# Reordering the opening of a fused transformer kernel: one transposing transfer ahead of two loads, one tile centred by halves

## The chip, the cores and the metric

The kernel runs on one core of one Trainium2 chip. The metric is the device time of one execution in microseconds (us). The granted TensorE clock was 1.0 in every run but one, a run at 0.998. A profiled execution gives a span about 2 us shorter than its time (1290.4 against 1292.35 for the profiled run of the kernel before).

Engines: PE is TensorE, DVE is VectorE, ACT is ScalarE, SP is the engine that issues all transfers here. "SPq" in a timeline is SP issuing a transfer; the transfer itself lands later.

## The reference, cut to what matters

Four layers over one activation of 2048 rows by 1024: attention, token-mixing MLP, attention, MLP.

```
x = x + A(layernorm(x), wqkv, wo)     # layer 1: V = layernorm(x) @ wqkv[:, 2048:3072], then Q, K, ...
x = x + B(layernorm(x), w1, b1, w2, b2)
x = x + A(layernorm(x), wqkv, wo)
x = x + B(layernorm(x), w1, b1, w2, b2)
```

The change touches only the first 35 us: load x in 16 tiles of 128 rows (256 KB each), normalise each, transpose each, and multiply by the V weights.

## The kernel before: the parts that matter

Each engine gets a list of work in a fixed order. `x_load k` loads tile k, `w_load kt` loads weight row kt of the V weights (256 KB), `S_`/`A_`/`R_`/`N_` take the statistics of a tile, its reciprocal root and normalise it, `M_`/`Ma` only centre it (tiles 0 and 1, whose scale is applied later), `tr` transposes on TensorE, `C_` copies the result from PSUM to `hT`, `T_ k` is a transposing transfer from the normalised tile into `hT`, `V_` is the projection, `E_` evicts it. `VV(k, kt, ...)` is the projection of tile k with the named weight rows alone, and `W_` is a matmul on dummy data.

```python
def T_(k):
    return nc.sync.dma_start_transpose(out=hT[:, :, cols(*order[k])], in_=xs[k])
...
pe = [(tr, 0, 0), (tr, 0, 1), (W_, 1), *VV(0, 0), (tr, 1, 0), (tr, 1, 1), *VV(0, 1, 2), *VV(1, 0, 1, 2)]
for kt in range(3, 6):
    pe += [*VV(0, kt), *VV(1, kt)]
pe += [(tr, 2, 0), (tr, 2, 1), *VV(0, 6, 7), *VV(1, 6, 7)]
pe += [(V_, k, n, a8) for k in range(2, NT) for n in range(NDC)]
act = [(Ma, 0, halves[1]), (C_, 0, 0), (C_, 0, 1), (C_, 1, 0), (C_, 1, 1), (R_, 0), (R_, 1), (R_, 2), (R_, 3), (C_, 2, 0),
       (C_, 2, 1), (R_, 4), (E_, 0), (R_, 5), (E_, 1), (R_, 6), (E_, 2), (E_, 3)]
rs = [(R_, k) for k in range(7, NT)]
for k in range(4, NT):          # E_4, R_7, R_8, E_5, R_9, R_10, E_6, ...
    act.append((E_, k))
    act += rs[:2]
    del rs[:2]
dve = [..., (S_, 1, 0), (S_, 1, 1), (A_, 1), (M_, 1, whole[0]), (S_, 2, 0), (S_, 2, 1), (A_, 2)]
...                             # then per tile k: S_ k+1 (first half), N_ k, S_ k+1 (second half), A_ k+1
sp = [(x_load, 0, halves), (x_load, 1), *((w_load, kt) for kt in range(4)), (x_load, 2), (w_load, 4), (w_load, 5),
      (x_load, 3), (w_load, 6), (w_load, 7), (x_load, 4), (x_load, 5), (x_load, 6), (T_, 3), (x_load, 7), (x_load, 8),
      (T_, 4), (x_load, 9), (x_load, 10), (x_load, 11), (T_, 5), (x_load, 12), (x_load, 13), (T_, 6), (x_load, 14),
      (x_load, 15), (T_, 7), (T_, 8), (T_, 9), (T_, 0), (T_, 1), *((T_, k) for k in range(10, NT)), (load_biases,)]
```

The softmax here doesn't subtract the row's maximum and nothing guards it: scores larger than these inputs give would overflow.

Of the kernel before, what the change touches and what calls it, by code (L numbers as in the profile page):

```python
# [25 lines left out]
def kernel(  # L26
# [177 lines left out]
    def chain_(eng, f, *args):  # L204
        with tc.issue_after(last[eng].ins) if eng in last else nullcontext():
            last[eng] = f(*args)

    def start_up(v, wv):
        xc = [x2(f"xc{k}") for k in range(2)]
        xs, tps, pss_, mvs, sts, rss = {}, {}, {}, {}, {}, {}  # L210
# [22 lines left out]
        def B_(k):  # L233
            return nc.vector.tensor_scalar(out=nm0[:], in0=mvs[k][:, 0:1], scalar1=-1.0, scalar2=None, op0=ALU.mult)

        def M_(k, h):
            return nc.vector.tensor_scalar(out=xc[k][:, h], in0=xs[k][:, h], scalar1=mvs[k][:, 0:1], scalar2=None,
                                           op0=ALU.subtract)

        def Ma(k, h):  # L240
            return nc.scalar.activation(out=xc[k][:, h], in_=xs[k][:, h], func=ACT.Identity, bias=nm0[:])

        def R_(k):
# [48 lines left out]
        halves = (slice(0, D // 2), slice(D // 2, D))  # L292
        whole = (slice(0, D),)
        chain_("ACT", ln_exp_table)
        def VV(k, *kts):
            return [(V_, k, n, [kt]) for kt in kts for n in range(NDC)]

        a8 = range(KD)
        pe = [(tr, 0, 0), (tr, 0, 1), (W_, 1), *VV(0, 0), (tr, 1, 0), (tr, 1, 1), *VV(0, 1, 2), *VV(1, 0, 1, 2)]
        for kt in range(3, 6):  # L300
            pe += [*VV(0, kt), *VV(1, kt)]
        pe += [(tr, 2, 0), (tr, 2, 1), *VV(0, 6, 7), *VV(1, 6, 7)]
        pe += [(V_, k, n, a8) for k in range(2, NT) for n in range(NDC)]
        act = [(Ma, 0, halves[1]), (C_, 0, 0), (C_, 0, 1), (C_, 1, 0), (C_, 1, 1), (R_, 0), (R_, 1), (R_, 2), (R_, 3), (C_, 2, 0),
               (C_, 2, 1), (R_, 4), (E_, 0), (R_, 5), (E_, 1), (R_, 6), (E_, 2), (E_, 3)]
        rs = [(R_, k) for k in range(7, NT)]
        for k in range(4, NT):
            act.append((E_, k))
            act += rs[:2]
            del rs[:2]  # L310
        dve = [(S_, 0, 0), (S_, 0, 1), (A_, 0), (B_, 0), (M_, 0, halves[0]), (S_, 1, 0), (S_, 1, 1), (A_, 1), (M_, 1, whole[0]),
               (S_, 2, 0), (S_, 2, 1), (A_, 2)]
        for k in range(2, NT):
            nx = k + 1 < NT
# [8 lines left out]
            if k in (8, 9):  # L323
# [1 line left out]
        dve.append((zero_fill,))  # L325
        dve.append((cast_biases,))
        sp = [(x_load, 0, halves), (x_load, 1), *((w_load, kt) for kt in range(4)), (x_load, 2), (w_load, 4), (w_load, 5),
              (x_load, 3), (w_load, 6), (w_load, 7), (x_load, 4), (x_load, 5), (x_load, 6), (T_, 3), (x_load, 7), (x_load, 8),
              (T_, 4), (x_load, 9), (x_load, 10), (x_load, 11), (T_, 5), (x_load, 12), (x_load, 13), (T_, 6), (x_load, 14),
              (x_load, 15), (T_, 7), (T_, 8), (T_, 9), (T_, 0), (T_, 1), *((T_, k) for k in range(10, NT)), (load_biases,)]  # L330
        qs = {"PE": pe, "ACT": act, "DVE": dve, "SP": sp}
        need = {cast_biases: lambda: (load_biases,) in done, R_: lambda k: k in mvs, N_: lambda k, h: k in rss, tr: lambda k, hf: (N_, k) in done if k > 1 else (M_ if k or not hf else Ma, k) in done,
                S_: lambda k, cc: (x_load, k) in done,
                B_: lambda k: k in mvs, M_: lambda k, h: k in mvs, Ma: lambda k, h: (B_, k) in done, C_: lambda k, hf: (k, hf) in tps,
                V_: lambda k, n, kts: ((C_, k, kts[-1] * 2 // KD) in done or (T_, k) in done), E_: lambda k: (V_, k, 1) in done and (k > 1 or k in rss),
                T_: lambda k: (N_, k) in done and (k > 1 or (E_, k) in done)}
        done = set()
        while any(qs.values()):
            for eng, q in qs.items():
                while q and (q[0][0] not in need or need[q[0][0]](*q[0][1:])):  # L340
                    f, *args = q.pop(0)
                    chain_(eng, f, *args)
                    if f is V_:
                        if args[2][-1] == KD - 1:
                            done.add((f, args[0], args[1]))
                    else:
                        done.add((f, *(args if f is C_ else args[:1])))

    def load_wv():
        return [wt_("wv", [P, 2, D]) for _ in range(KD // 2)]  # L350
# [280 lines left out]
    for li in range(2):  # L631
# [5 lines left out]
        if first:  # L637
            start_up(v, wv)
            wts = [None, None]
            chain_("SP", load_qk, 0, wts)  # L640
            res = lambda c, i: xin_v[c, i]
        else:
            fill_wv(wv)
            wts = [None, None]
            chain_("SP", load_qk, 0, wts)
            for i in range(NI):
                for c in range(DIL):
                    v_proj(v, c, i, wv, (0, 1))
            res = lambda c, i: rows(xb, c, i)
# [104 lines left out]
```

## Time and profile before

| | kernel before |
|---|---|
| median time before the prediction, 3 runs | 1292.2 us (1292.11 to 1293.29) |
| profiled span | 1290.4 us |
| TensorE busy | 1285.0 us |
| TensorE idle before tile 1's transposes | 0.75 us |
| TensorE idle before tile 4's projection | 0.64 us shown; 0.80 us counted from 22.05, where 32 matmuls of 0.216 us after 15.14 end |

The page of the profile says what limits the kernel. These are the first lines of its first part (busy time, share, number of instructions) and of the chain of waits that ended last:

```profile
span 1290.4 us, 19531 instructions
PE 1285.0 (100%) x8422; PEld 591.8 (46%) x8422; DVE 417.4 (32%) x854; ACT 368.7 (29%) x609; POOL 2.4 (0%) x15
...
PE 98%; DMA 1%; DVE 0%; SPq 0%; ACT 0%; issue 0%
```

TensorE is busy all the time, so a reordering can win only its idle time, 5.4 us, of which most is at the very start and the very end. The Trainium skill ("Perfetto Trace Analysis", section "Identifying the Most-Contended Engine") warns that matmul busy time does not say how near a kernel is to its roofline; it is enough here, since the change removes no matmul and only gaps can move.

The timeline of TensorE before. Columns: start, duration, engine, line, operation, output <- inputs, shape, count, and in brackets the idle time before it and what ended it:

```profile
7.76 0.62 PE L256 MATMUL m<-ident,xc 128*128 128x128 bf16 x8 [0.75 <-DVE xc L237]
...
15.14 7.07 PE L267 MATMUL s<-wv,hT 128*128 128x512 bf16 x32
22.85 3.63 PE L267 MATMUL acc<-wv,hT 128*128 128x512 bf16 x16 [0.64 <-DMA hT<-x]
26.31 7.07 PE L267 MATMUL s<-wv,hT 128*128 128x512 bf16 x32
33.22 3.62 PE L267 MATMUL acc<-wv,hT 128*128 128x512 bf16 x16
...
64.30 7.07 PE L375 MATMUL m<-hT,wqk 128*128 128x512 bf16 x32
```

The line at 7.76 is tile 1's transposes, 15.14 is tiles 2 and 3, 22.85 is tile 4, 26.31 tiles 5 and 6, 33.22 tile 7, and 64.30 the first matmul of the Q/K projection. The two gaps are in brackets.

The same stretch of SP, as it issues loads (DMA_DIRECT2D, L218) and transposing transfers (L279):

```profile
14.86 1.36 SPq L279 DMA_TRANSPOSE hT<-x  x1
16.28 1.05 SPq L218 DMA_DIRECT2D x<-in_A_x_dram  x2
17.43 1.24 SPq L279 DMA_TRANSPOSE hT<-x  x1
...
23.93 1.24 SPq L279 DMA_TRANSPOSE hT<-x  x1
25.21 1.08 SPq L218 DMA_DIRECT2D x<-in_A_x_dram  x2
28.56 18.66 SPq L279 DMA_TRANSPOSE hT<-x  x11
```

A duration here is the time SP spends issuing. The Trainium skill says so ("Perfetto Trace Analysis", section "DMA Instruction — HWDGE (DVE, Sync)"): the profiled window ends when the issuer is free, and the data's movement is not in it. This trace agrees: tile 4's transfer shows 1.24 us from 17.43, and its data landed 5.4 us after that start. The view of one tile (here the transfers into `hT` that were issued in a short window around 17.43) gives the landing:

```profile
L279 SPq DMA_TRANSPOSE hT<-x x1: 1237/1237/1237, 17.4 to 17.4; - x1
...
DMA to landing us min/median/max: 5.4/5.4/5.4
```

17.43 and 5.4 make 22.8, which is where TensorE resumes. The same view around 28.56 gives tile 7's transfer in the kernel before; it matters later:

```profile
L279 SPq DMA_TRANSPOSE hT<-x x1: 1238/1238/1238, 28.6 to 28.6; - x1
...
DMA to landing us min/median/max: 3.1/3.1/3.1
```

It landed at 31.7, and TensorE reached tile 7 at 33.22: 1.5 us to spare.

### The profile page before, as it was taken

How to read it: one execution, taken by the hardware profiler on the slowest of the kernel's cores; microseconds unless marked ns; L12 is line 12 of the kernel's file. 1: busy time of each engine (PE TensorE's matmuls, PEld its weight loads, DVE VectorE, ACT ScalarE, POOL GpSimd, SP SyncE). 2: the span in 40 equal slices, each digit the busy share in tenths (PEclk: the TensorE clock that was granted, in tenths of full speed). 3: DMA queues.
4: the chain of work that ended last, by engine and by line, in shares of the span. 5: the costliest groups of instructions: out<-in, count | busy, mean ns of one | idle time of the engine just before them, and what ended most of it. 6: DMA issues, size and time to landing. Idle time of an engine off the chain costs nothing.

```text
span 1290.4 us, 19531 instructions
## 1 busy us (share of the span) xinstructions
PE 1285.0 (100%) x8422; PEld 591.8 (46%) x8422; DVE 417.4 (32%) x854; ACT 368.7 (29%) x609; POOL 2.4 (0%) x15
## 2 busy tenths in 40 slices
PE   9999999999999999999999999999999999999999
PEld 4444444444444444444444444444444444444444
DVE  6566777820000022322300677678000000111111
ACT  4366664541111110000023666645311111000000
POOL 0000000000000000000000000000000000000000
PEclk9999999999999999999999999999999999999999
DMA  8611124642222244465410111247323222334330
GB/s 240 112 46 48 50 83 124 208 139 82 66 82 75 57 117 132 131 164 132 131 32 1 48 49 51 80 151 218 116 67 91 72 62 81 102 106 136 118 92 33
DMA packets 204102, 126.59 MB, mean 98 GB/s; under 512 B 44272, under 2 KB 183792, under 8 KB 204016
## 3 DMA queue, kind: packets, MB, share of 16 engines
q1 hardware_dynamic: 204016, 125.35, 34.3%
q8 instruction: 66, 1.08, 0.4%
q14 instruction: 20, 0.16, 0.0%
HBM read 96.48 MB, written 16.78 MB: 88 GB/s over the span
## 4 chain that ended last, share of the span: by engine, by line
PE 98%; DMA 1%; DVE 0%; SPq 0%; ACT 0%; issue 0%
PE m L375 18%; PE s L617 15%; PE s L570 15%; PE m L490 9%; PE acc L570 7%; PE acc L617 7%; PE m L570 7%; PE m L617 7%; PE m L360 4%; PE s L267 2%; PE s L406 2%; PE acc L441 1%; PE acc L267 1%; PE acc L445 1%; DMA x<-in_A_x_dram 0%; DMA hT<-x 0%
## 5 line engine op out<-in xcount | busy, mean ns | idle before, releaser
L617 PEld LDWEIGHTS <-w 128*128 128x128 bf16 x1820 | 177.0, 98 | 210.2
L570 PEld LDWEIGHTS <-w 128*128 128x128 bf16 x1792 | 175.4, 98 | 211.4
L375 PE MATMUL m<-hT,wqk 128*128 128x512 bf16 x1024 | 231.8, 380 | 0.0
L570 PE MATMUL s<-h,w 128*128 128x512 bf16 x896 | 202.9, 379 | 0.0
L617 PE MATMUL s<-g,w 128*128 128x512 bf16 (+1 forms) x924 | 201.6, 374 | 0.0
L619 DVE SCALAR_TENSOR_TENSOR xo<-s,b_sb,xs 128x512 bf16<-128x512 f32 (+1 forms) x33 | 24.4, 739 | 532.9 <-PE s L617 528.7
L375 PEld LDWEIGHTS <-wqk 128*128 128x128 bf16 x1024 | 95.2, 98 | 118.0 <-issue 10.7
L421 DVE TENSOR_TENSOR Pm<-pc,band 32x640 bf16<-32x640 bf16 x256 | 123.6, 483 | 56.2 <-ACT pc L409 49.3
L490 PE MATMUL m<-wo,oT 128*128 128x512 bf16 x512 | 111.5, 379 | 0.0
L570 PE MATMUL acc<-h,w 128*128 128x512 bf16 x448 | 103.9, 379 | 0.0
L617 PE MATMUL acc<-g,w 128*128 128x512 bf16 x448 | 100.6, 379 | 0.0
L570 PE MATMUL m<-h,w 128*128 128x512 bf16 x448 | 99.0, 379 | 0.0
L617 PE MATMUL m<-g,w 128*128 128x512 bf16 (+1 forms) x448 | 97.8, 376 | 0.0
L178 ACT ACTIVATE ln<-mv,eps 128x1 f32<-128x1 f32 x64 | 18.8, 294 | 228.7 <-DVE mv L186 184.9
L490 PEld LDWEIGHTS <-oT 128*128 128x128 bf16 x512 | 49.6, 98 | 60.4 <-issue 1.3
L577 ACT ACTIVATE g<-s,b_sb 128x1024 bf16<-128x1024 f32 x28 | 31.2, 1113 | 158.2 <-PE s L570 158.2
L386 DVE COPY qB<-qs 32x512 bf16<-32x512 bf16 x136 | 38.2, 281 | 95.3 <-ACT qs L382 94.0
L360 PE MATMUL m<-wv,hT 128*128 128x512 bf16 x256 | 55.4, 379 | 0.0
L409 ACT ACTIVATE pc<-s,shift 128x640 bf16<-128x640 f32 x64 | 51.1, 799 | 11.7 <-PE s L406 11.7
L382 ACT CAST qs<-m 128x512 bf16<-128x512 f32 x64 | 37.4, 585 | 48.4 <-PE m L375 48.4
L379 ACT CAST kT<-m 128x512 bf16<-128x512 f32 x64 | 37.5, 586 | 46.5 <-PE m L375 46.5
L497 DVE TENSOR_TENSOR xn<-m,xr 128x512 bf16<-128x512 f32 x64 | 44.2, 690 | 16.9 <-PE m L490 16.8
(67 smaller groups left out, 678.9 us busy)
## 6 DMA issues: line engine op xcount, KB each, us to landing
w<-in_B_w_dram SPq DMA_DIRECT2D x56, 512.0 KB, 3.8
w<-in_B_w_dram SPq DMA_DIRECT2D x64, 448.0 KB, 4.4
wqk<-in_A_wqkv_dram SPq DMA_DIRECT2D x16, 512.0 KB, 4.8
xa<-xn SPq DMA_DIRECT2D x32, 256.0 KB, 2.2
xs<-xa SPq DMA_DIRECT2D x32, 256.0 KB, 3.1
wo<-in_A_wo_dram SPq DMA_DIRECT2D x8, 512.0 KB, 5.4
xr<-in_A_x_dram SPq DMA_DIRECT2D x16, 256.0 KB, 3.3
xb<-xo SPq DMA_DIRECT2D x16, 256.0 KB, 2.7
```

The costliest lines, as they stand in the source:

```text
L267: r = nc.tensor.matmul(pss_[k][:, n, :], lhsT=hT[:, kt, cols(*order[k])], rhs=wv[kt // 2][:, kt % 2, n * 512:(n + 1) * 512], start=(kt == ...
L360: nc.tensor.matmul(ps[:], lhsT=hT[:, kt, cols(c, i)], rhs=wv[kt // 2][:, kt % 2, n * 512:(n + 1) * 512], start=(kt == 0), stop=(kt == KD - 1))
L375: mm = nc.tensor.matmul(ps[:], lhsT=wts[part][:, kt, (g % 2) * P:(g % 2 + 1) * P], rhs=hT[:, kt, lo:lo + 512], start=(kt == 0), stop=(kt = ...
L379: nc.scalar.copy(out=kT[u % 2][:, ls], in_=ps[:])
L382: nc.scalar.copy(out=qs[:], in_=ps[:])
L386: nc.vector.tensor_copy(out=qB[u % 2][hp, h, ls], in_=qs[hp, :])
L409: nc.scalar.activation(out=pc[:].rearrange("p (n t) h k -> p n (t h k)", n=2), in_=ss[:, :, 0:2 * HG * GW], func=ACT.Exp, scale=scale, bia ...
L421: mm = nc.vector.tensor_tensor(out=Pm[rp, :, s0:s0 + HB, r * KG:r * KG + GW].rearrange("p h t k -> p t h k"), in0=pc[rp], in1=mk, op=ALU.mult)
L490: mm = nc.tensor.matmul(ps[:], lhsT=oT[g][:, cols(c, i)], rhs=wo[n][g // 4][:, g % 4, :], start=(g == 0), stop=(g == NG - 1))
L497: return nc.vector.tensor_tensor(out=xn[:, xs_], in0=pss_["o", n][:], in1=xr[:, xs_], op=ALU.add)
L570: nc.tensor.matmul(pairs[fl][0][dc], lhsT=wt[c][:, i, fl * P:(fl + 1) * P], rhs=h2[c][i][:, dc * 512:(dc + 1) * 512], start=(k == 0), stop ...
L617: nc.tensor.matmul(ap, lhsT=w2t[ft // HF][:, ft % HF, c::DIL], rhs=g[ft // GF][:, ft % GF, lo:lo + w], start=(ft == 0), stop=(ft == FT - 1))
```

## The change

The intent: close both gaps. Tile 4's transposing transfer goes right behind tile 3's, ahead of two loads, and the later loads are regrouped. Tile 1 is centred in two halves, so that its transposes can start after the first, and two matmuls of tile 0 are put ahead of the transposes to fill the gap.

```diff
-        pe = [(tr, 0, 0), (tr, 0, 1), (W_, 1), *VV(0, 0), (tr, 1, 0), (tr, 1, 1), *VV(0, 1, 2), *VV(1, 0, 1, 2)]
+        pe = [(tr, 0, 0), (tr, 0, 1), (W_, 1), *VV(0, 0, 1), (tr, 1, 0), (tr, 1, 1), *VV(0, 2), *VV(1, 0, 1, 2)]
-        dve = [..., (A_, 1), (M_, 1, whole[0]), ...
+        dve = [..., (A_, 1), (M_, 1, 0), (M_, 1, 1), ...
-              ... (x_load, 6), (T_, 3), (x_load, 7), (x_load, 8),
-              (T_, 4), (x_load, 9), (x_load, 10), (x_load, 11), (T_, 5), (x_load, 12), (x_load, 13), (T_, 6), (x_load, 14),
-              (x_load, 15), (T_, 7), (T_, 8), ...
+              ... (x_load, 6), (T_, 3), (T_, 4), (x_load, 7),
+              (x_load, 8), (x_load, 9), (T_, 5), (x_load, 10), (x_load, 11), (T_, 6), (x_load, 12), (x_load, 13), (x_load, 14),
+              (x_load, 15), (T_, 7), (T_, 8), ...
 # cut: M_ and Ma take the number of a half, and the bookkeeping of what is done knows halves
```

More of the change, by code (lines that the diff above doesn't have):

```diff
@@ L234, in B_, with M_, Ma @@
             return nc.vector.tensor_scalar(out=nm0[:], in0=mvs[k][:, 0:1], scalar1=-1.0, scalar2=None, op0=ALU.mult)
-        def M_(k, h):
+        def M_(k, hf):
+            h = halves[hf]
             return nc.vector.tensor_scalar(out=xc[k][:, h], in0=xs[k][:, h], scalar1=mvs[k][:, 0:1], scalar2=None,
                                            op0=ALU.subtract)
-        def Ma(k, h):
+        def Ma(k, hf):
+            h = halves[hf]
             return nc.scalar.activation(out=xc[k][:, h], in_=xs[k][:, h], func=ACT.Identity, bias=nm0[:])
@@ L303, in start_up @@
         pe += [(V_, k, n, a8) for k in range(2, NT) for n in range(NDC)]
-        act = [(Ma, 0, halves[1]), (C_, 0, 0), (C_, 0, 1), (C_, 1, 0), (C_, 1, 1), (R_, 0), (R_, 1), (R_, 2), (R_, 3), (C_, 2, 0),
+        act = [(Ma, 0, 1), (C_, 0, 0), (C_, 0, 1), (C_, 1, 0), (C_, 1, 1), (R_, 0), (R_, 1), (R_, 2), (R_, 3), (C_, 2, 0),
                (C_, 2, 1), (R_, 4), (E_, 0), (R_, 5), (E_, 1), (R_, 6), (E_, 2), (E_, 3)]
@@ L310, in start_up @@
             del rs[:2]
-        dve = [(S_, 0, 0), (S_, 0, 1), (A_, 0), (B_, 0), (M_, 0, halves[0]), (S_, 1, 0), (S_, 1, 1), (A_, 1), (M_, 1, whole[0]),
+        dve = [(S_, 0, 0), (S_, 0, 1), (A_, 0), (B_, 0), (M_, 0, 0), (S_, 1, 0), (S_, 1, 1), (A_, 1), (M_, 1, 0), (M_, 1, 1),
                (S_, 2, 0), (S_, 2, 1), (A_, 2)]
@@ L327, in start_up @@
         sp = [(x_load, 0, halves), (x_load, 1), *((w_load, kt) for kt in range(4)), (x_load, 2), (w_load, 4), (w_load, 5),
-              (x_load, 3), (w_load, 6), (w_load, 7), (x_load, 4), (x_load, 5), (x_load, 6), (T_, 3), (x_load, 7), (x_load, 8),
-              (T_, 4), (x_load, 9), (x_load, 10), (x_load, 11), (T_, 5), (x_load, 12), (x_load, 13), (T_, 6), (x_load, 14),
+              (x_load, 3), (w_load, 6), (w_load, 7), (x_load, 4), (x_load, 5), (x_load, 6), (T_, 3), (T_, 4), (x_load, 7),
+              (x_load, 8), (x_load, 9), (T_, 5), (x_load, 10), (x_load, 11), (T_, 6), (x_load, 12), (x_load, 13), (x_load, 14),
               (x_load, 15), (T_, 7), (T_, 8), (T_, 9), (T_, 0), (T_, 1), *((T_, k) for k in range(10, NT)), (load_biases,)]
         qs = {"PE": pe, "ACT": act, "DVE": dve, "SP": sp}
-        need = {cast_biases: lambda: (load_biases,) in done, R_: lambda k: k in mvs, N_: lambda k, h: k in rss, tr: lambda k, hf: (N_, k) in done if k > 1 else (M_ if k or not hf else Ma, k) in done,
+        need = {cast_biases: lambda: (load_biases,) in done, R_: lambda k: k in mvs, N_: lambda k, h: k in rss, tr: lambda k, hf: (N_, k) in done if k > 1 else (M_, k, hf) in done,
                 S_: lambda k, cc: (x_load, k) in done,
-                B_: lambda k: k in mvs, M_: lambda k, h: k in mvs, Ma: lambda k, h: (B_, k) in done, C_: lambda k, hf: (k, hf) in tps,
+                B_: lambda k: k in mvs, M_: lambda k, hf: k in mvs, Ma: lambda k, hf: (B_, k) in done, C_: lambda k, hf: (k, hf) in tps,
                 V_: lambda k, n, kts: ((C_, k, kts[-1] * 2 // KD) in done or (T_, k) in done), E_: lambda k: (V_, k, 1) in done and (k > 1 or k in rss),
@@ L346, in start_up @@
                     else:
-                        done.add((f, *(args if f is C_ else args[:1])))
+                        done.add((M_ if f is Ma else f, *(args if f in (C_, M_, Ma) else args[:1])))
     def load_wv():
```

## The prediction

> **What bounds the kernel.** The page's first part has TensorE busy 1285.0 of 1290.4 us, clock 1.0; the chain of waits is 98% TensorE. Only its idle time can be removed by a reordering. The timeline shows all of it: 1.05 us at the start, 0.15 and 0.08 us around the first transposes, 0.75 us before tile 1's transposes (7.01 to 7.76, released by VectorE's centring), 0.64 us before tile 4's first projection matmul (22.85, released by the transposing DMA), and 2.65 us after the last matmul. The change aims at the last two of the opening: at most 1.4 us, 0.1% of the run.
>
> **Part 1, tile 4's transfer.** Tile 4 is normalised at 16.27+0.55 = 16.82, but its transfer is issued at 17.43, behind two loads that start issuing at 16.28, and takes 5.4 us to land (22.80). Tile 3's, on an idle queue, took 3.2 us (14.86 to 18.06). The Trainium skill, "DMA: Bandwidth & Descriptors", section "Queues, rings and completion order", says each DMA engine consumes its descriptors in ring order; the 5.4 against 3.2 us agrees: tile 4 queued behind 512 KB of loads. Changed: issue near 16.87, landing at 20.1 to 20.6. TensorE needs it at about 21.7 (below), so the wait goes entirely. TensorE really stood from 22.05 (32 matmuls of 0.216 us from 15.14) to 22.85: 0.80 us.
>
> **Part 2, tile 1.** The two moved matmuls need weight row 1: issued 2.67, landed 4.2 later, 6.87; they run 6.9 to 7.35 inside the gap. The first half of the centring (0.34 us, as tile 0's half took) ends at 7.56 rather than 7.71, so the transposes start near 7.60; the second half ends near 7.85. Two halves cost VectorE about 0.15 us more, harmless: it then waits until 9.57 for tile 2. ScalarE's copy of the first half ends near 8.6, so tile 1's matmuls start near 8.67, not 9.08: 0.4 us gained, with a new stop of about 0.15 us. Weights 3 to 7 (landing 8.4 to 12.8) and tile 2's normalisation (12.25) still come in time. Tile 2's copy follows tile 3's reciprocal root on ScalarE (13.72 to 14.25) and cannot start before 14.16; tile 2's matmuls therefore start near 14.78 instead of 15.14: 0.36 us survives.
>
> **Sum.** Alone, part 2 would be worth nothing, since tile 4's landing absorbs it. With part 1, tile 4's matmuls start near 14.78+6.91 = 21.7, not 22.85: 1.15 us gained.
>
> **Given back?** Tile 5's transfer issues near 19.7 (before 21.48), lands near 24.2; needed at 25.1. Tile 7's load now lands near 22.4, not 19.6, and VectorE's statistics for it stand before tile 6's normalisation: tile 6's transfer slips to near 23.4, lands near 27.5; needed at 28.6. Tile 7 follows ScalarE's eviction of tile 4, which itself is earlier. So no new wait, with about 1 us to spare. After that TensorE has no gap until the end, and the gain is carried to it.
>
> **Predicted:** 1291.1 us, range 1290.5 to 1292.0. Faster by over 2%: 0.005; within 2%: 0.99; slower by over 2%: 0.005.
>
> **Signs.** Timeline: no idle before tile 4's matmuls, which start near 21.7; tile 4's transfer issued near 16.9, landing 3.2 to 3.8 us later; the 0.75 us gap split into about 0.3 us and a small stop before tile 1's matmuls; the V projection ends near 63.1 instead of 64.3; the groups' means unchanged.
>
> **What would make it wrong.** Tile 4's transfer landing after 21.7; tile 3's (18.06) coming after TensorE's earlier need at 18.24; weight row 1 landing later than 7.0, so that the moved matmuls delay tile 1's transposes; tile 5 or 6 landing late because the loads were pushed behind; or run-to-run spread (1292.11 to 1293.29 before) as large as the gain.

## The result

| | before | changed |
|---|---|---|
| median of 6 runs | 1292.35 us (1292.11 to 1293.29) | 1292.49 us (1291.95 to 1293.31) |
| profiled span | 1290.4 us | 1289.9 us |

The ratio is 1.0001, with a 95% interval of 0.9988 to 1.0014: the same. Ratios in this document are the mean time of one kernel's fast runs over that of the other's of the same rounds, so not quite the ratio of the medians quoted. The prediction was 1291.1, and the median lies outside its range of 1290.5 to 1292.0.

The first part of the profile's page after:

```profile
span 1289.9 us, 19532 instructions
PE 1285.3 (100%) x8422; PEld 592.0 (46%) x8422; DVE 417.6 (32%) x855; ACT 369.2 (29%) x609; POOL 2.4 (0%) x15
```

The timeline of TensorE after, for the same pieces of work as above:

```profile
7.41 0.61 PE L258 MATMUL m<-ident,xc 128*128 128x128 bf16 x8
...
14.65 7.08 PE L269 MATMUL s<-wv,hT 128*128 128x512 bf16 x32
21.57 3.62 PE L269 MATMUL acc<-wv,hT 128*128 128x512 bf16 x16
25.02 7.07 PE L269 MATMUL s<-wv,hT 128*128 128x512 bf16 x32
32.64 3.63 PE L269 MATMUL acc<-wv,hT 128*128 128x512 bf16 x16 [0.55 <-DMA hT<-x]
...
63.73 7.07 PE L377 MATMUL m<-hT,wqk 128*128 128x512 bf16 x32
```

Both gaps are gone, and tile 4 starts at 21.57 instead of 22.85, 1.28 us sooner: a little better than predicted. But a new line is in brackets. Tile 7 (32.64) waits for its transposing transfer, which it did not do before. It could have started 32 matmuls of 0.216 us after 25.02, at 31.93. So 0.71 us of the 1.28 is given back there, and 0.57 us (64.30 to 63.73) is left in this trace.

SP and the landing of tile 7's transfer after:

```profile
14.73 3.22 SPq L281 DMA_TRANSPOSE hT<-x  x2
18.00 2.60 SPq L218 DMA_DIRECT2D x<-in_A_x_dram  x3
...
23.16 1.24 SPq L281 DMA_TRANSPOSE hT<-x  x1
24.45 2.08 SPq L218 DMA_DIRECT2D x<-in_A_x_dram  x4
27.27 17.78 SPq L281 DMA_TRANSPOSE hT<-x  x11
```

```profile
L281 SPq DMA_TRANSPOSE hT<-x x1: 1244/1244/1244, 27.3 to 27.3; - x1
...
DMA to landing us min/median/max: 5.3/5.3/5.3
```

Tile 7's transfer is issued 1.29 us sooner than before (27.27 against 28.56), as foreseen, but it lands 5.3 us after that instead of 3.1, at 32.6 instead of 31.7. The four loads just ahead of it (24.45 to 26.53) are the suspect. Note that the same nine loads, of tiles 7 to 15, stand ahead of tile 7's transfer in both lists. What differs is when they land: the last at 30.1 before, 1.5 us ahead of the transfer's own landing, and at 31.7 after. One reason can be read off the times of SP: it issues in order, tile 4's transfer had to wait for its tile until 16.71, and so the load of tile 7 behind it was issued at 18.00 instead of 16.28.

### The profile page after: what moved, and what is told of

It reads as the page before. It is cut to its first block, busy times and chain, and to the rows that moved or that the text cites. A ratio compares the mean times of both kernels' runs of the same rounds, so it can differ in the third digit from the quotient of the medians.

```text
span 1289.9 us, 19532 instructions
## 1 busy us (share of the span) xinstructions
PE 1285.3 (100%) x8422; PEld 592.0 (46%) x8422; DVE 417.6 (32%) x855; ACT 369.2 (29%) x609; POOL 2.4 (0%) x15
## 4 chain that ended last, share of the span: by engine, by line
PE 99%; DMA 1%; DVE 0%; ACT 0%; issue 0%
PE m L377 18%; PE s L619 15%; PE s L572 15%; PE m L492 9%; PE acc L619 7%; PE acc L572 7%; PE m L572 7%; PE m L619 7%; PE m L362 4%; PE s L269 2%; PE s L408 2%; PE acc L269 1%; PE acc L443 1%; PE acc L447 1%; DMA hT<-x 0%; DMA x<-in_A_x_dram 0%
## 5 line engine op out<-in xcount | busy, mean ns | idle before, releaser
L499 DVE TENSOR_TENSOR xn<-m,xr 128x512 bf16<-128x512 f32 x64 | 44.2, 690 | 16.9 <-PE m L492 16.8
```

Source lines behind the costliest of these rows:

```text
L499: return nc.vector.tensor_tensor(out=xn[:, xs_], in0=pss_["o", n][:], in1=xr[:, xs_], op=ALU.add)
```

## The experiments

Theory: in the changed order tile 7's transfer stands behind four loads that were issued just before it, and it lands when they have. Rivals: the transfer is late because what it waits for on ScalarE is late; the total traffic of the opening is the limit, whatever the order; or the first trace was a lucky or unlucky one.

Twelve experiments ran in three batches, each batch beside the kernel before on a chip of its own (nine runs of before in each batch: medians 1292.56, 1292.39 and 1292.25). All twelve were correct.

### 1. The transfers alone

```diff
 # pe, dve as in the kernel before; sp as in the change
```

> Only the order of the transfers is the change's; tile 1 as before. My theory (tile 7's transfer now queues behind four loads and lands near 32.6 us whatever TensorE does): tile 4's matmuls start near 22.1 with no wait for its transfer, tile 7's matmuls still start near 32.6 to 33.0 with 0.2 to 0.6 us of wait for the transfer; the Q/K projection starts 63.7 to 64.1 (before 64.30, the change 63.73); time 0.2 to 0.6 us under before. Rival (tile 7's transfer is late only because tile 4's eviction and the root behind it are late, with a fixed 5.3 us of landing): its landing moves with tile 4's matmuls, to 33.1 or later.

Measured: median 1292.03 (1291.42 to 1293.03), ratio 0.9997 [0.9984, 1.0009]. The profiled run was its slowest, span 1291.0:

```profile
21.47 3.62 PE L267 MATMUL acc<-wv,hT 128*128 128x512 bf16 x16
...
33.80 3.63 PE L267 MATMUL acc<-wv,hT 128*128 128x512 bf16 x16 [1.61 <-ACT v L276]
```

The wait at tile 7 is there without the tile 1 part. The bracket names ScalarE, but the eviction that tile 7 needs (of tile 4, which used the same buffer) was over at 26.13; a wait for several semaphores is put down to whatever the profile saw last. The landing says what it was:

```profile
L279 SPq DMA_TRANSPOSE hT<-x x1: 1247/1247/1247, 27.2 to 27.2; - x1
...
DMA to landing us min/median/max: 6.6/6.6/6.6
```

27.2 and 6.6 make 33.8. The transfer was issued 0.1 us sooner than in the change and landed 1.2 us later, so a fixed landing time behind a late issue is excluded. My numbers missed on both sides: tile 4 started at 21.47 rather than 22.1, and tile 7 later than 33.0.

### 2. Tile 1 alone

```diff
 # pe, act, dve as in the change; sp as in the kernel before
```

> Only tile 1's part of the change (halves, two matmuls ahead); transfers in the order of before. My theory: tile 2's matmuls start near 14.65 instead of 15.14, but tile 4's wait for its transfer grows from 0.64 to about 1.1 us and its matmuls start at 22.7 to 22.9 as before; Q/K projection from 64.2 to 64.3; time equal to before within 0.2 us. Rival (the tile 1 part is worth 0.5 us by itself): Q/K projection from 63.8, time 0.5 us less.

Measured: median 1292.81 (1292.49 to 1293.18), ratio 1.0003 [0.999, 1.0015]. TensorE:

```profile
14.91 7.08 PE L269 MATMUL s<-wv,hT 128*128 128x512 bf16 x32
23.17 3.63 PE L269 MATMUL acc<-wv,hT 128*128 128x512 bf16 x16 [1.18 <-DMA hT<-x]
```

As the theory had it, what is gained before tile 2 is lost again at tile 4, whose transfer landed at 23.1 and whose wait grew from 0.64 to 1.18 us. Alone, this part is worth nothing. The numbers missed here too: tile 2 started at 14.91 and not near 14.65, and tile 4 at 23.17, later than expected and later than before.

### 3 and 9. The change again, twice

> The changed kernel once more, five rounds beside before on one chip, to see whether the 0.5 us of the trace shows in the times and whether tile 7's wait returns. Theory: wait of 0.4 to 1.0 us before tile 7's matmuls at 32.4 to 32.9, Q/K projection from 63.6 to 64.0, time 0.5 us under before, interval about 0.1% wide, so not told from equal. Rival (the trace was a lucky one): no gain in a second trace, Q/K projection at 64.2 or later.

> The changed kernel a third time. Theory (all that differs between runs lies ahead of tile 7's matmuls; span minus the start of those was 1257.2 to 1257.3 us in all ten traces so far): span = that start + 1257.2; wait at tile 7 of 0.5 to 1.7 us; times spread over 1 us or more; mean 0 to 0.7 us under before. Rival (noise sits elsewhere, in the long part after): the difference leaves 1257.1 to 1257.4.

Measured: third run of the list, median 1291.64 (1291.19 to 1292.65), ratio 0.9994 [0.9981, 1.0008]; ninth, median 1292.21 (1291.10 to 1293.43), ratio 1.0002 [0.9988, 1.0016]. In both traces tile 7 waits, and starts at 33.06 and 32.89. The brackets name other releasers again, so the landing was looked up: 33.0 and 32.8. The second trace is less good than I expected: tile 7 at 33.06 rather than up to 32.9, Q/K projection at 64.16 rather than up to 64.0, just short of the rival's 64.2. The five times beside it are 0.6 us under before in the mean, those of the ninth 0.2 us over, where I had expected 0 to 0.7 under.

Span minus the start of tile 7's matmuls is 1257.24 and 1257.21 here, and lies between 1257.18 and 1257.26 in all fourteen traces. So nothing that differs between these kernels, or between profiled runs of one kernel, happens after the start of tile 7. With that, the span of each unprofiled run gives an estimate of when tile 7 started: from 31.8 to 34.0 us over 15 of the change's 16 runs. (The run at clock 0.998 is left out: its later part need not have taken 1257.2 us.) The times spread by 2.3 us (1291.10 to 1293.43), and their mean (the first six, and five each here) is 1292.32, or 1292.24 without that run; the mean of the 24 runs of before beside them is 1292.40. Nothing was won that stands clear of this spread.

### 4. Two of the four loads behind tile 7's and 8's transfers

```diff
-(T_, 6), (x_load, 12), (x_load, 13), (x_load, 14), (x_load, 15), (T_, 7), (T_, 8), (T_, 9),
+(T_, 6), (x_load, 12), (x_load, 13), (T_, 7), (T_, 8), (x_load, 14), (x_load, 15), (T_, 9),
```

> The changed kernel with the loads of tiles 14 and 15 issued behind the transfers of tiles 7 and 8, so two loads stand between tile 6's and tile 7's transfers and not four. My theory (loads ahead in the queue): tile 7's transfer lands 3.2 to 4.0 us after issue at 27.3, by 31.3; TensorE goes from tile 6 to tile 7 at 31.9 with no wait; Q/K projection from 63.0; profiled span 1289.2, time 1.1 to 1.3 us under before. Rival (bytes only moved about: the chain of transfers is bound by throughput to 32.5): tile 7 still waits 0.5 us, Q/K projection from 63.7.

Measured: median 1291.38 (1291.14 to 1291.75), ratio 0.9992 [0.9979, 1.0005]. Tile 7's transfer landed 4.7 us after 27.29 (expected 3.2 to 4.0), at 32.0, and tile 7 started at 32.45 without a wait:

```profile
21.59 3.62 PE L269 MATMUL acc<-wv,hT 128*128 128x512 bf16 x16
25.24 7.37 PE L269 MATMUL s<-wv,hT 128*128 128x512 bf16 x32
32.45 3.62 PE L269 MATMUL acc<-wv,hT 128*128 128x512 bf16 x16
```

The gain is 1.04 us in the means of this batch. But it is smaller than it could be in this trace. Tile 5 starts 0.2 us late (16 matmuls after 21.59 end at 25.04), and the 32 matmuls of tiles 5 and 6 take 7.37 us, not 7.07: tile 6's transfer, behind two loads issued just before, landed 5.2 us after 23.74, when TensorE was already there. So those transfers have next to no slack either, and my estimate of 1 us to spare was wrong for them too. It also means that this trace is a weak test of tile 7: had TensorE lost nothing at tiles 5 and 6, it would have reached tile 7 at 31.96, just as the transfer landed (31.98).

### 5 and 6. One load between two transfers, with and without the tile 1 part

```diff
-(T_, 4), (x_load, 7), (x_load, 8), (x_load, 9), (T_, 5), (x_load, 10), (x_load, 11), (T_, 6), (x_load, 12), (x_load, 13), (x_load, 14), (x_load, 15), (T_, 7), (T_, 8), (T_, 9), (T_, 0), (T_, 1), ...
+(T_, 4), (x_load, 7), (T_, 5), (x_load, 8), (x_load, 9), (T_, 6), (x_load, 10), (T_, 7), (x_load, 11), (T_, 8), (x_load, 12), (T_, 9), (x_load, 13), (T_, 0), (x_load, 14), (T_, 1), (x_load, 15), ...
 # 5: pe, act, dve as in the change; 6: as in the kernel before
```

> The change, but with the loads of tiles 7 to 15 dealt out, one (once two) between two transfers, so no transfer of tiles 4 to 9 has more than two loads ahead. Theory (a transfer lands about 1 us after the load issued just ahead of it, so late loads cost nothing and early ones do): tile 5's, 6's and 7's transfers land before 24, 27.5 and 31; TensorE runs from 14.7 to the end of the opening without a wait; Q/K projection from 63.0; span 1289.2; time 1.0 to 1.4 us under before, and the five times closer together than the change's. Rival (total traffic is the limit): some transfer among tiles 5 to 10 is late again by 0.3 us or more.

> As the run before, with tile 1 as in the kernel before. The traces so far: where tile 1's data landed at 5.1 to 5.3 us the old code lost nothing at tile 1 (14.56 for tile 2's matmuls), where it landed at 5.6 it lost 0.3 us (15.14 against 14.78 and 14.91). Theory: 0 to 0.4 us slower than the run before by the landing of tile 1's data, mean 0.2. Rival (prediction's view of the tile 1 part as a sure 0.36 us): 0.36 us slower in the mean.

Measured: the first, median 1291.38 (1291.02 to 1291.44), ratio 0.9992 [0.998, 1.0005]; the second, median 1291.02 (1290.87 to 1291.55), ratio 0.9991 [0.9977, 1.0005]. TensorE of the first has no wait for a transfer:

```profile
21.34 3.62 PE L269 MATMUL acc<-wv,hT 128*128 128x512 bf16 x16
24.79 7.07 PE L269 MATMUL s<-wv,hT 128*128 128x512 bf16 x32
31.70 3.62 PE L269 MATMUL acc<-wv,hT 128*128 128x512 bf16 x16
```

The second has the same regular steps (14.70, 21.61, 25.06, 31.97). Transfers 5, 6 and 7 landed at 23.2, 26.7 and 30.1 in the first. The same bytes are moved in all, so the total traffic is not the limit (but fewer are ahead of tile 7's transfer: loads 11 to 15 come after it). The times also lie closer together: within 0.42 and 0.68 us, where the change spreads over 1.4 to 2.2, its run at clock 0.998 left out.

The kernel without the tile 1 part is not slower; its mean is 0.17 us lower, within the scatter. So the sure 0.36 us of the prediction is refuted, and no gain of the tile 1 part shows in times. The traces say why. In the first trace of before, tile 1's data landed at 5.6 and the gap was 0.75 us. In experiments 1 and 6, with the same code for tile 1, VectorE began on it at 5.08 and 5.21; the gap before the transposes was 0.07 and 0.19, and tile 2 started at 14.56 and 14.70. (In experiment 10, below, it is 5.35, 0.54 and 14.96.) With the changed code tile 2 started between 14.33 and 14.91 in ten traces, 14.61 in the mean, against 14.84 in the four with the old code. So the part may bring 0.2 us on average, which is too little to show in these times. Over all fourteen traces VectorE began on tile 1 by 5.35 in eleven; the landing at 5.6 that made the gap 0.75 us wide was the rarer case.

### 7 and 11. No load between tile 6's and tile 7's transfers

```diff
-(T_, 6), (x_load, 12), (x_load, 13), (x_load, 14), (x_load, 15), (T_, 7), (T_, 8), (T_, 9),
+(T_, 6), (T_, 7), (T_, 8), (x_load, 12), (x_load, 13), (x_load, 14), (x_load, 15), (T_, 9),
```

> The change with all four loads (tiles 12 to 15) behind tile 8's transfer: none between the transfers of tiles 6 and 7. Landing of tile 7's transfer so far: four loads between 5.3, 5.5 and 6.6 us, two loads 4.7. Theory: 3.1 to 3.6 us as for tile 3's on an idle queue, landing near 30.6; no wait at tile 7. Rival (late because tile 6's transfer and the loads before it are still draining): 4.5 us or more.

> The order with no load between the transfers of tiles 6 and 7, now timed beside the change on one chip. Theory: no wait at tile 7 (start 31.6 to 32.2), times 1.1 to 1.4 us under before and 0.6 to 1.2 us under the change, within 0.5 us of each other. Rival (the single 1290.89 was a lucky run): no faster than the change.

Measured: 1290.89 in the one run; then, with five, median 1291.19 (1290.98 to 1291.78), ratio 0.9994 [0.9981, 1.0006]. In the same batch the change's mean is 1292.42 and this kernel's 1291.36, 1.05 us less (0.80 without the run at clock 0.998), and 0.86 less than before, where I had expected 1.1 to 1.4. The five times span 0.8 us, more than the 0.5 expected. Tile 7's transfer, issued at 27.2 as in the change:

```profile
L281 SPq DMA_TRANSPOSE hT<-x x1: 1232/1232/1232, 27.2 to 27.2; - x1
...
DMA to landing us min/median/max: 3.0/3.0/3.0
```

Tile 7 starts at 31.59 and 31.88 in the two traces, without a wait. This is the cleanest test: the transfer is issued at nearly the same time as in the change (26.94 and 27.22), only the four loads have moved behind it, and the wait is gone. So with four loads just ahead it took 5.3 to 6.6 us, with two 4.7 and 5.4 (experiments 4 and 12), with none 3.0. It is not the count alone: two loads issued 2.3 us ahead cost nothing in the kernel before (3.1 us). What fits all of these is when the loads ahead land: in all fourteen traces tile 7's transfer landed 3.0 us after its issue or 1.0 us after the last load ahead of it, whichever came later, within 0.1 us.

### 8. Tile 2's load ahead of weight row 3

```diff
-(x_load, 1), *((w_load, kt) for kt in range(4)), (x_load, 2), (w_load, 4), ...
+(x_load, 1), *((w_load, kt) for kt in range(3)), (x_load, 2), (w_load, 3), (w_load, 4), ...
 # the rest as in experiment 5
```

> As the first run of this batch, and tile 2's load ahead of weight row 3. Theory: tile 2's matmuls are paced by tile 2's landing (they start 5.0 to 5.3 us after VectorE begins on tile 2 at 9.2 to 9.7, in the traces where TensorE did not pace them), so landing 0.4 us sooner brings them to 14.5, where TensorE itself is the limit: 0.1 to 0.3 us under the first run of this batch. Rival (weight row 3 becomes late): TensorE stands before the matmuls of row 3 near 9.8 and nothing or less is gained.

Measured: median 1291.28 (1290.89 to 1291.89), ratio 0.9992 [0.9979, 1.0005]; mean equal to experiment 5's. VectorE did begin on tile 2 sooner (8.50 against 9.22 us), and weight row 3 was not late, but tile 2's matmuls started at 14.71, paced by TensorE's own work, which had begun later in this run. A miss: nothing gained, neither theory supported.

### 10. The kernel before again

> The kernel before once more, for its trace. Theory: tile 4 waits again for its transfer (0.3 to 1.3 us, tile 4's matmuls at 22.5 to 23.3), no wait at tile 7 (33 to 33.7); the gap before tile 1's transposes is 0.75 us only if tile 1's data lands at 5.6, and 0 to 0.3 us if it lands at 5.1 to 5.3; span minus tile 7's start 1257.2. Rival (the first trace of before was typical in all): gap of 0.7 us again whatever the landing.

Measured: one run, span 1291.0. Tile 4 waited 1.37 us for its transfer and started at 23.41; tile 7 started at 33.78 without a wait. The gap before tile 1's transposes was 0.54 us with tile 1's data in at 5.35, between the cases I had named. Before, too, scatters with the landing of a transfer, tile 4's.

### 12. Tile 4's move alone

```diff
 # pe, act, dve as in the change
-(T_, 3), (T_, 4), (x_load, 7), (x_load, 8), (x_load, 9), (T_, 5), (x_load, 10), (x_load, 11), (T_, 6), (x_load, 12), (x_load, 13), (x_load, 14), (x_load, 15), (T_, 7),
+(T_, 3), (T_, 4), (x_load, 7), (x_load, 8), (x_load, 9), (x_load, 10), (x_load, 11), (T_, 5), (x_load, 12), (x_load, 13), (T_, 6), (x_load, 14), (x_load, 15), (T_, 7),
```

> The change, but of the transfers only tile 4's moves ahead of two loads; after it loads 7 to 11 all stand ahead of tile 5's transfer, and the rest is as before. Theory (late by the loads ahead in the queue): tile 5's transfer now comes last behind five loads, issued near 22, landing 4 to 5 us later near 26 to 27; TensorE waits 1 to 2 us at tile 5 (ready at 25.1) and tile 7 has no wait of its own; span 1290 to 1291. Rival (tile 7 is late through tile 4 being early): tile 7 waits here too.

Measured: one run, 1293.21, span 1291.1 (0.1 over what I expected):

```profile
21.42 3.62 PE L269 MATMUL acc<-wv,hT 128*128 128x512 bf16 x15
27.00 7.08 PE L269 MATMUL s<-wv,hT 128*128 128x512 bf16 x32 [1.96 <-DMA hT<-x]
33.91 3.62 PE L269 MATMUL acc<-wv,hT 128*128 128x512 bf16 x15
```

(Some matmul records are missing from this trace; x15 is tile 4's and tile 7's 16.) The wait moves to the tile whose transfer stands behind the most loads: tile 5, behind five, landed at 27.0. Tile 7 shows no wait, but this does not decide against the rival, because TensorE came to it 2 us late, at 33.91. Its transfer was as late as in the change:

```profile
L281 SPq DMA_TRANSPOSE hT<-x x1: 1243/1243/1243, 27.2 to 27.2; - x1
...
DMA to landing us min/median/max: 5.4/5.4/5.4
```

That is 32.6, with only two loads between it and tile 6's transfer, and without the wait at tile 5 TensorE would have been there at 31.8 (48 matmuls of 0.216 us after 21.42). So it is not the number of loads between the two transfers that counts, but how late the loads ahead land: the last landed at 31.6 here. In the traces with tile 4's transfer early and all loads still ahead of tile 7's (the change, 1 and 12) the last one landed at 31.6 to 32.8, in those with the old order (before, 2 and 10) at 29.6 to 30.1. Experiments 2 and 12 differ in nothing but the place of tile 4's transfer, and there it is 29.6 against 31.6 (one trace each): with this transfer in front, the loads come late, and whatever stands behind them comes late too. Where the last four or five of them are behind tile 7's transfer (5 to 8 and 11), tile 4's is early and tile 7's in time.

## Why the prediction was wrong

- **Tile 4's transfer: right.** Predicted issue near 16.9, landing 3.2 to 3.8 us later; measured 16.7 and 3.2. The wait at tile 4 vanished in every kernel with the early transfer.
- **Tile 4's matmuls: right in this trace.** Predicted 21.7, measured 21.57, and between 21.23 and 21.68 in every trace with the early transfer.
- **The tile 1 part: wrong as a sure gain.** "0.36 us survives" rested on one trace, in which tile 1's data landed late. In most traces it lands sooner, and where it was in by 5.2 the old code waited 0.2 us or less. The times of experiments 5 and 6 show no gain; the traces suggest 0.2 us on average.
- **"Given back?": the step that failed.** The prediction said: "Tile 7 follows ScalarE's eviction of tile 4, which itself is earlier. So no new wait, with about 1 us to spare." The first half held: the transfer was issued 1.29 us sooner. What I left out was that the regrouped list puts four loads between tile 6's and tile 7's transfers, issued from 2.8 to 0.7 us ahead of it, and that the last of them lands at 31.7, with the transfer about 1 us behind it. I costed tile 7's issue and not its landing, though I had used exactly this effect to explain tile 4's 5.4 us: it landed 5.3 us after its issue instead of 3.1, at 32.6, 0.7 us after TensorE's need at 31.93. Experiments 7 and 11 put the loads behind it and the wait goes; experiments 5 and 6 do so with most of them, with the same result.
- **Tiles 5 and 6: right only just.** Tile 6: predicted landing 27.5 with 28.6 needed; measured 28.3 with 28.5 needed, and in experiment 4 it was late. Tile 5: predicted 24.2 with 25.1 needed; measured 24.75 with 25.02 needed.
- **The size.** Predicted gain 1.15 us, trace 0.57 us, times 0.08 us (1292.40 to 1292.32 in the means of all runs). The change turned a wait at tile 4 of 0.6 to 1.4 us (two traces) into a wait at tile 7 of 0.6 to 0.9 us (three traces), with a wider spread. The three traces of the change had starts of tile 7 of 32.64 to 33.06; by the estimate above its runs went up to 34.0. That the first six runs showed no gain at all where one trace showed 0.57 fits this spread; which transfer was late in the runs that were not profiled, nothing shows.
- **After the opening: right.** "After that TensorE has no gap until the end, and the gain is carried to it": 1257.2 us from tile 7 to the end in all traces.

What stays open: why the landing of the same transfer behind the same four loads varies from 5.3 to 6.6 us, and why the first loads of a run land up to half a microsecond apart (VectorE began on tile 1 between 5.07 and 5.66). No experiment addressed the source of that scatter. The DMA packets in the traces narrow it. A load is moved in packets of 2048 B, a transposing transfer in packets of 256 B, which take 0.018 us in the median. In the four traces with all four loads just ahead of tile 7's transfer (the change's three and experiment 1), 18 to 22 of the small packets took far longer, the longest 0.5, 1.0, 2.1 and 2.0 us, and ended nearly together; tile 7's transfer landed 1.1 to 1.2 us after that. Most of the DMA then stood still: experiment 9 moved 52 GB/s from 30.0 to 31.5 us, against 352 in the 1.5 us before 29.5. The same is seen at tile 4 in both traces of the kernel before (17 packets, up to 1.6 us, ended at 21.8 and 22.4, landing 1.0 us later). So a transposing transfer that had begun was held up by something. Every trace also has one 16 KB packet of the instruction queue, 1.0 to 1.9 us long, between 18.5 and 22.1 us; whether that is where the delay starts was not tested.

The experiments point to a better version: the change's early tile 4 with the loads dealt out (experiments 5 and 6) or held behind tile 8's transfer (11). Their means are 0.9 to 1.3 us under before's of the same batch; in experiment 11 also 1.05 us under the change. That is 0.1%: by the intervals still the same, but nearly all runs lie below all of before's.

## What to carry to other kernels

When transfers share one queue, cost a moved transfer by when the loads ahead of it will land and not only by its own issue, and do this for every transfer behind it in the list, not only for the one that is moved; a load moved back for one tile is a load moved in front of another, and a transfer that waits for its tile holds back every load behind it in the list. Deal loads out between the transfers that feed the busy engine, as late as their own users allow. And when the gain is under the run-to-run spread, take several traces before believing a gap: here one of the two gaps was half an accident of one run.

## What the Trainium skill lacked or had wrong

- "DMA: Bandwidth & Descriptors", section "Queues, rings and completion order", says that each DMA engine consumes its descriptors in ring order. The runs agree, and give a size that the page lacks: a transposing transfer of 256 KB landed 3.0 to 3.2 us after its issue with no load waiting ahead, and otherwise mostly about 1 us after the last load ahead of it had landed (tile 7 in the change: load in at 31.7, transfer at 32.6; tile 5 in experiment 12: 25.5 and 27.0; but tile 4 in experiment 2: 20.7 and 23.1).
- The same page, section "Latency and other measured facts", gives a transposing transfer 261 GB/s, and 350 to 400 GB/s when contiguous. Here the slices in which tile 7's transfer ran alone (experiment 11, 28.5 to 29.6 us) show 193 to 240 GB/s, from SBUF to SBUF. Its destination, `hT[:, :, cols]`, is not contiguous, so the first figure is the one to compare, and the measured rate is below it.
- No page has the time that a transposing transfer of this size costs its issuer on this chip ("DMA: Bandwidth & Descriptors" has only sequencer cycles for other sizes, in its part on a later chip): 1.23 to 1.37 us of SP here when nothing held it up, against about 0.43 us for a plain load of the same size. Behind a filled queue both grow: the third load after tile 4's transfer took 1.5 to 2.4 us to issue in the traces of the change, and tile 8's transfer 2.2 to 2.5. "Perfetto Trace Analysis", section "DMA Instruction — HWDGE (DVE, Sync)", draws a descriptor buffer that fills; that this is the cause was not tested.
- No page says how far the landing of the same loads differs from run to run: within the change's three traces VectorE began on tile 1 at 5.13, 5.22 and 5.66, and tile 7's transfer landed at 32.6, 32.8 and 33.0; the change could win about 1.2 us.
